# Order of the first rows of a Fourier layer, and operands of a seven-product matmul formed two steps sooner

## The chip, the cores and the metric

The kernel runs on one core of a Trainium2 chip. Its engines are TensorE (PE in the profile; PEld are its weight loads), VectorE (DVE), ScalarE (ACT), GpSimd (POOL), and SyncE (SP), which here only issues DMAs. Each takes its instructions in program order; they meet through semaphores. An engine that waits for one instruction does not pass to the next. The metric is the device time of one execution, in microseconds.

## The reference

Two sublayers, each with a layer norm, a modulation of the normalized rows, and a gated residual; S = 2048 rows, D = 512, F = 1792.

```
mod = silu(c) @ w_mod                      # six rows sa, ca, ga, sb, cb, gb
h = layernorm(x) * (1 + ca) + sa
a, b = h @ Wd_re.T, h @ Wd_im.T
x = x + ga * (Ws_re @ a - Ws_im @ b)       # Fourier mixing
h = layernorm(x) * (1 + cb) + sb
z = gelu(h @ w_in)                         # 512 -> 1792
z1, z2 = z[:, :896], layernorm(z[:, 896:])
g = w_sp @ z2 + b_sp                       # 2048 x 2048
x = x + gb * ((z1 * g) @ w_out)
```

All is float32.

## The kernel before

**Three products for one.** TensorE works on a reduced float type. Each operand is split into a high part (ScalarE copies it to that type) and a low part (VectorE subtracts the high part from the original). `matmul3` (L93 to L97) then makes three matmuls: high by high, and the two mixed ones. L95, L96 and L97 in the profile are these three. `ah` and `al` are the high and low parts of the streamed chunk (`prep_hi`, L289 for the high part; `prep_lo`, L307 for the low part); a chunk is 128 x 512.

**Order.** The order of every engine's instructions is written out by hand. The work counts through chunks n. For each, `prep(n)` emits the high part of chunk n+3 and the low part of chunk n+2, then come the matmuls, then what `at(n, ...)` has put on the list for n. N2 = 128 is the first chunk of z1, N3 the first of z2, N4 the first of the big product with w_sp.

**The head.** Stage one multiplies the normalized rows (without the modulation, which is folded into other operands) by the sequence matrices. A row block s of x (128 rows) becomes the stationary operand: `stats_first(s)` takes mean and variance on VectorE (L423 to L426) and then the power and the scaled shift on GpSimd (L427, L428, tile `first`). `norm_x(s)` makes the normalized rows `xn` on ScalarE (L119) after GpSimd has filled their column 0 with ones (L468). The high part `hh` comes in one of two ways. `hi_first(s)` makes it straight from x, with scale and shift inside one activation (L444), and then writes the one column of ones (L446). `hi_h(s)` copies it from `xn` (L477). `lo_h(s)` subtracts on VectorE: `hl` = xn - hh (L482). The streamed chunk is a 32 x 32-block transpose on VectorE of a block of the sequence matrix (`t`, L190, from `stage`). Block 0 holds chunks 0 to 3. Block 1, the first of the second matrix, holds chunks 4 to 7; its load is issued ahead of all this. For the first four chunks `mm_a` (L501) runs three passes of four matmuls: hh by ah, hh by al, hl by ah.

The head before gives row blocks 0 and 1 to `hi_first` and 2 and 3 to `hi_h`.

**z1 with seven products.** The product of h with the left half of `w_in` uses a seven-product scheme (Strassen's, in Winograd's form) over two halves of the features and two halves of the rows. Four quarters g of 512 rows each have four chunks of 128 features: `TT[k, g]`. Half gg pairs quarter gg with quarter 2+gg. With a = TT[kk, gg], b = TT[2+kk, gg], c = TT[kk, 2+gg] and d = TT[2+kk, 2+gg] the scheme needs the difference a - c and S2 = d - (a - c), and later a + S2 (`sum_x11`) and b - S2 (`sum_x12`). Products run in the order 1, 2, 6, 7, 4, 5, 3, each in two steps of two chunks, one for each half: step n (even) uses chunks n and n+1. A step has 18 matmuls into three banks (`z1p`). Product 6 uses S2, product 7 uses a + S2, product 5 uses the difference, which lies where c was.

Around a step, in the program's order (`mm_z1`): the matmuls; the high parts of the two chunks four ahead (`ahead`); the emptying of the banks. For product 1 and for 6 and 7 the emptying is a copy (L772). For product 2 it is, for each bank, a gelu out of it (L731, `z1o`) and a refill with product 1 (L759, `z1p<-z`). After that stand the low parts of the same two chunks. The weights of product p are formed by `form_v`, split by `hi_v` (L658) and `lo_v` (L662), and kept in two buffers `vj`.

The left half has 896 columns: 2 x 384 go through the scheme, the last 128 (`f7p`, weights `w7`) are multiplied plainly. For quarters 2 and 3 this needs the original c in high and low parts (`make_x`: `xh` L218, `xl` L221). `mm_x` runs these 12 matmuls, 6 behind step 6 and 6 behind step 12.

**Where these things lie and when.** The quarters 2 and 3 are loaded by `load_t` (L209) into numbered slots of 2 KB per partition, a pool opened at the start of z1 where the Fourier stage's weight pool (`htpool`: 19 tiles of 2 KB and one of 0.5 KB) and its neighbours were. Before, in `make_x(0)` xh and xl of half 0 lie in slots 9 to 12, and VectorE alternates: xl, difference, xl, difference. The difference goes into the slot of c (L223). `form_t` forms S2 (L245) inside `prep_hi`, that is directly ahead of the high part of the chunk that uses it: two chunks of four ahead of product 6's step. For half 1, `make_d` (L234) writes the differences into the buffers `bh`, `bl` of a third pool at step 6.

Stores of finished z1 rows (`z_d<-z1o`, L734) are issued by GpSimd. The copies of product 6 go into the buffers of product 2's rows once they are stored. Loads of w_sp blocks (`sj`, L833) are issued by SP from step 6 on.

Of the kernel before, what the change touches and what calls it, by code (L numbers as in the profile page):

```python
# [8 lines left out]
F32 = mybir.dt.float32  # L9
F32R = mybir.dt.float32r  # L10
AF = mybir.ActivationFunctionType
ALU = mybir.AluOpType

P = 128
# [5 lines left out]
def fnet_gmlp_kernel(  # L20
# [32 lines left out]
    nc = tc.nc  # L53
# [3 lines left out]
    Q = 512  # L57
# [5 lines left out]
    x = x.rearrange("b s d -> (b s) d")  # L63
# [59 lines left out]
    def at(n, f, *a):  # L123
        fill.setdefault(n, []).append((f, a))
# [14 lines left out]
    N2 = 4 * len(src)  # L139
# [61 lines left out]
    def slot(i, name, dtype=F32):  # L201
        return slots[0].tile([P, Q], dtype, tag=f"slot{i}", bufs=1, name=name)
# [3 lines left out]
    def load_t(g):  # L206
        for k in range(ND):
            TT[k, g] = slot(1 + 4 * (g - 2) + k, f"tt{g}_{k}")
            nc.sync.dma_start(TT[k, g], ht_d[g][k * P:(k + 1) * P, :])  # L209

    def make_x(gg):

        if gg:
            XH[gg] = [[bpool[0].tile([P, Q], F32R, tag=m, bufs=3, name=f"x{m}{kk}") for m in ("bh", "bl")] for kk in range(2)]
        else:
            XH[gg] = [(slot(9 + kk, f"xh{gg}{kk}", F32R), slot(11 + kk, f"xl{gg}{kk}", F32R)) for kk in range(2)]
        for kk, (h, _) in enumerate(XH[gg]):
            nc.scalar.activation(h, TT[kk, 2 + gg], AF.Copy)  # L218
        for kk, (h, l) in enumerate(XH[gg]):
            t = TT[kk, 2 + gg]  # L220
            nc.vector.tensor_tensor(l, t, h.bitcast(F32), op=ALU.subtract)  # L221
            if not gg:
                nc.vector.tensor_tensor(t, TT[kk, gg], t, op=ALU.subtract)  # L223
        if gg:
            for kk in range(2):
                TT[kk, 3] = XD[kk]

    XD = []

    def make_d():  # L230

        for kk in range(2):
            XD.append(bpool[0].tile([P, Q], F32, tag=("bh", "bl")[kk], bufs=3, name=f"xd{kk}"))
            nc.vector.tensor_tensor(XD[kk], TT[kk, 1], TT[kk, 3], op=ALU.subtract)  # L234

    def form_t(n):

        stage1 = n < N3
        p = (YPROD if stage1 else ZPROD)[(n - (N2 if stage1 else N3)) // 4]
        gg, kk = divmod(n % 4, 2)  # L240
        a, b, c, d = TT[kk, gg], TT[2 + kk, gg], TT.get((kk, 2 + gg)), TT.get((2 + kk, 2 + gg))
        if p == 6:
            if stage1:
                S2[gg, kk] = slot(13 + 2 * gg + kk, f"s2_{gg}{kk}")
                nc.vector.tensor_tensor(S2[gg, kk], d, XD[kk] if gg else c, op=ALU.subtract)  # L245
            return S2[gg, kk]
        if stage1:
            return {1: a, 2: b, 7: a, 4: b, 5: c, 3: d}[p]
        if p in (1, 2):
            t = blocks.tile([P, Q], F32, tag="t", bufs=2, name=f"t{n}")  # L250
            nc.vector.tensor_tensor(t, a if p == 1 else b, S2[gg, kk], op=ALU.subtract if p == 1 else ALU.add)
            return t
        return {7: c, 4: d, 5: a, 3: b}[p]
# [18 lines left out]
    def prep_hi(n):  # L272
        if n >= NE or n in highs:
            return
        highs.add(n)
        if N2 <= n < N4:
            T[n] = form_t(n)
        else:
            b, k = divmod(n, 4) if n < N2 else (NB0 + (n - N4) // 4, (n - N4) % 4)
            if b != NB0:  # L280
                T[n] = blocks.tile([P, Q], F32, tag="t", bufs=2, name=f"t{n}")
            if b == NB0:
                assert n in T
            elif n >= N4:
                squares(T[n], stage[b][:, k % 2], k // 2)
            else:
                squares(T[n], stage[b], k)
        AH[n] = SE[2][:, n - N4] if N4 <= n < N4 + 4 else blocks.tile([P, Q], F32R, tag="ah", bufs=4, name=f"ah{n}")
        nc.scalar.activation(AH[n], T[n], AF.Copy)  # L289
        if not N2 <= n < N4 and k == 3:  # L290
            stage.pop(b)
            if b != NB0:
                load(b + 2)


    def prep_lo(n):
        if n >= NE or n in lows:
            return
        lows.add(n)
        if N2 <= n < N4 and n % 4 == 3:  # L300
            AL[n] = slot(0, f"al{n}", F32R) if slots else zrow[0].tile([P, Q], F32R, tag="z1u", bufs=6, name=f"al{n}")
        elif N4 <= n < N4 + 4:
            AL[n] = slot(9 + n - N4, f"al{n}", F32R)
        else:
            AL[n] = blocks.tile([P, Q], F32R, tag="al", bufs=3, name=f"al{n}")
        t = T.pop(n)
        nc.vector.tensor_tensor(AL[n], t, AH[n].bitcast(F32), op=ALU.subtract)  # L307
# [112 lines left out]
    def stats_first(s):  # L420

        m = spool.tile([P, 12], F32, tag="first", bufs=4, name=f"first{s}")
        nc.vector.bn_stats(m[:, :6], X[s])  # L423
        mv = m[:, 8:]
        nc.vector.bn_aggr(mv[:, :2], m[:, :6])
        nc.vector.tensor_scalar(mv[:, 1:2], mv[:, 1:2], EPS, None, op0=ALU.add)  # L426
        nc.gpsimd.tensor_tensor(mv[:, 2:3], mv[:, 1:2], mhalf, op=ALU.pow)  # L427
        nc.gpsimd.tensor_scalar(mv[:, 3:4], mv[:, 0:1], mv[:, 2:3], -1.0, op0=ALU.mult, op1=ALU.mult)  # L428
        NRM[s] = mv[:, 2:3], mv[:, 3:4]
# [11 lines left out]
    def hi_first(s):  # L441
        h_hi[s] = hpool.tile([P, ND, P], F32R, name=f"hh{s}")
        h = h_hi[s].rearrange("p k (a i) -> p k a i", i=32)
        nc.scalar.activation(h, X[s].rearrange("p (a k i) -> p k a i", a=4, i=32), AF.Identity,  # L444
                             bias=NRM[s][1], scale=NRM[s][0])
        nc.scalar.activation(h_hi[s][:, 0, :1], ones[:, :1], AF.Copy)  # L446
# [16 lines left out]
    def norm_x(s):  # L463

        if s not in LN:
            LN[s] = spool.tile([P, D], F32, tag="xn", bufs=4, name=f"xn{s}")
        if s > 1:
            nc.gpsimd.memset(LN[s][:, 0:1], 1.0)  # L468
        apply(LN[s][:, 1:], X.pop(s)[:, 1:], NRM.pop(s))
# [5 lines left out]
    def hi_h(s):  # L475
        h_hi[s] = hpool.tile([P, ND, P], F32R, name=f"hh{s}")
        nc.scalar.activation(*parts_h(s, h_hi), AF.Copy)  # L477

    def lo_h(s):
        h_lo[s] = hpool.tile([P, ND, P], F32R, name=f"hl{s}")  # L480
        lo, h = parts_h(s, h_lo)
        nc.vector.tensor_tensor(lo, h, parts_h(s, h_hi)[0].bitcast(F32), op=ALU.subtract)  # L482
        LN.pop(s)
# [172 lines left out]
    def hi_v(p):  # L656
        WJ[1, p] = wpool[0].tile([P, 2, 2, Q], F32R, tag="wj", bufs=2, name=f"vj{p}")
        nc.scalar.activation(WJ[1, p][:, 0, :, :FM], v_of(p), AF.Copy)  # L658
# [56 lines left out]
    def end_f7(g):  # L715
        end_z1(g, NF - 1, ZT.pop(("f7", g)), out_row(g, NF - 1))
# [23 lines left out]
    def mm_z1(n):  # L740
        p = YPROD[(n - N2) // 4]
        gg = n % 4 // 2
        fresh = p in (1, 5)
        a = [(AH.pop(m), AL.pop(m)) for m in (n, n + 1)]
        if p in (2, 3):
            for kk, t in enumerate(a):
                mm_f7(gg if p == 2 else 2 + gg, 2 + kk, *t)
        for f in range(3):
            if fresh:
                ZT[gg, f] = bank(3 * gg + f, f"z1p{p}_{gg}{f}")  # L750
            cols = slice(f * P, (f + 1) * P)
            for kk, (th, tl) in enumerate(a):
                matmul3(ZT[gg, f], WJ[1, p][:, 0, kk, cols], WJ[1, p][:, 1, kk, cols], th, tl,
                        fresh and kk == 0, kk == 1, not fresh)
        ahead(n)
        for f in range(3):
            empty_z1(p, gg, f)
            if p == 2:
                nc.scalar.activation(turned(ZT[gg, f]), natural(Z1.pop((1, gg, f))), AF.Copy)  # L759
        if p == 1:  # L760
            for kk, t in enumerate(a):
                mm_f7(gg, kk, *t)
        if p == 2 and gg:
            hi_v(7)
            end_f7(1)

    def empty_z1(p, gg, f):
# [249 lines left out]
    stats_first(1)  # L1017
    prep_lo(0)
    norm_x(0)
    hi_first(1)  # L1020
    prep_hi(1)
    lo_h(0)
    stats_first(2)
    prep_lo(1)
    norm_x(1)
    lo_h(1)
    norm_x(2)
    hi_h(2)
    prep_hi(2)
    stats_first(3)  # L1030
    norm_x(3)
    at(0, lo_h, 2)
    at(0, hi_h, 3)
    at(1, lo_h, 3)
    at(0, load_x, 1, range(2, 4))
    at(2, load_row)
# [7 lines left out]
    for s, n in ((4, 4), (5, 4), (6, 6), (7, 6), (8, 10), (9, 10)):  # L1044
        m = n + (s == 9)
# [117 lines left out]
    at(N2 + 1, load_wi, 1, 2)  # L1163
    at(N2 + 2, form_v, 6)
    at(N2 + 3, load_t, 3)
    at(N2 + 4, make_x, 0)
    at(N2 + 6, make_d)
    at(N2 + 8, sum_x11, 0)
    at(N2 + 10, sum_x11, 1)
    at(N2 + 12, sum_x12, 0)  # L1170
    at(N2 + 14, sum_x12, 1)
    at(N2 + 13, form_v, 5)
    at(N2 + 17, form_v, 3)
    for i, p in enumerate(YPROD[2:]):
        if p != 7:
            at(N2 + 4 + 4 * i - (not i), hi_v, p)
        at(N2 + 5 + 4 * i - 2 * (not i), lo_v, p)
    at(N2 + 10, make_x, 1)
    at(N2 + 20, form_w, 7)
    at(NY[3], hi_w, 1)  # L1180
    at(NY[3] + 1, lo_w, 1)
# [162 lines left out]
```

## Time and profile before

| | |
|---|---|
| median of 3 runs | 941.92 us (941.4 to 942.54) |
| the profiled execution | 941.69 us |
| its span, first to last instruction | 939.9 us |
| granted clock of TensorE | 1.000 |
| busy: TensorE, VectorE, ScalarE, GpSimd | 931.0, 737.3, 414.3, 195.9 us |
| z1 on the span's time axis | 448.2 to 519.4 us |

Times in rows are microseconds from the span's start, and the second number is the length. `x2` at the end of a row means two instructions of the same kind, merged. Square brackets give the idle time of the engine ahead of the instruction and what ended it. A row `A <- B: total, times, longest` is an engine that waited for another. A matmul is listed with the time until its last result; the next one starts earlier than that.

### The profile page before, as it was taken

Reading aid. Unit: us, or ns where it says so; the run is one execution under the profiler, and the core shown is the slowest. Engines: PE = TensorE matmul, PEld = TensorE weight load, DVE = VectorE, ACT = ScalarE, POOL = GpSimd, SP = SyncE. Lnnn points to the kernel's source line nnn. Section 1 sums busy time; section 2 is a strip of 40 time slices with the busy share of each in tenths; the row PEclk is TensorE's granted clock in tenths of the full one; section 3 lists DMA queues with packets and bytes.
Section 4 is the critical chain, followed back from the end, with each engine's and each line's share of the span. In section 5 each row is a group of like instructions: output and inputs, shape, how many; then the busy total and the mean of one; then the engine's idle time right before and its main releaser. Section 6 shows DMA issues by size and latency. Waiting matters only on the chain.

```text
span 939.9 us, 12367 instructions
## 1 busy us (share of the span) xinstructions
PE 931.0 (99%) x4112; PEld 771.6 (82%) x4112; DVE 737.3 (78%) x1203; ACT 414.3 (44%) x728; POOL 195.9 (21%) x370
## 2 busy tenths in 40 slices
PE   8999999999999999999999999999999999999998
PEld 5888888888888888888878999888888888888886
DVE  6789957778677677875889878899799889886662
ACT  5685424232132222222488678674545544331221
POOL 2330000114554165323424211332000000000000
PEclk9999999999999999999999999999999999999999
DMA  9995762647539977994777523344564466744551
GB/s 204 226 224 123 144 145 68 168 135 183 141 86 303 294 212 215 277 336 147 234 279 271 183 92 74 92 100 104 130 140 107 114 145 135 179 112 145 183 176 56
DMA packets 236656, 157.08 MB, mean 167 GB/s; under 512 B 131536, under 2 KB 203472, under 8 KB 236464
## 3 DMA queue, kind: packets, MB, share of 16 engines
q1 hardware_dynamic: 222016, 118.39, 50.9%
q0 software_dynamic: 12128, 37.11, 11.0%
q10 hardware_dynamic: 2448, 0.79, 0.3%
q8 instruction: 32, 0.52, 0.2%
q14 instruction: 32, 0.26, 0.1%
HBM read 119.54 MB, written 36.70 MB: 166 GB/s over the span
## 4 chain that ended last, share of the span: by engine, by line
PE 92%; DVE 3%; ACT 2%; issue 1%; POOL 1%; DMA 0%; ACTq 0%; DVEq 0%; POOLq 0%
PE gp L96 12%; PE gp L97 12%; PE gp L95 12%; PE gw L95 10%; PE gw L96 10%; PE gw L97 10%; PE op L97 3%; PE op L96 3%; PE op L95 3%; PE yp L97 3%; PE yp L95 3%; PE yp L96 3%; PE z2p L96 2%; PE z2p L97 2%; PE z2p L95 2%; PE z1p L97 1%
## 5 line engine op out<-in xcount | busy, mean ns | idle before, releaser
L289 ACT ACTIVATE ah<-t 128x512 fp32r<-128x512 f32 x244 | 154.0, 632 | 370.3 <-DVE t L190 244.0
L307 DVE TENSOR_TENSOR al<-t,ah 128x512 fp32r<-128x512 f32 x244 | 164.0, 673 | 63.5 <-PE gp L96 37.5
L95 PE MATMUL gp<-ah,hh 128*128 128x512 f32 x496 | 193.0, 389 | 0.0
L97 PE MATMUL gp<-ah,hl 128*128 128x512 f32 x496 | 193.0, 389 | 0.0
L96 PE MATMUL gp<-al,hh 128*128 128x512 f32 x496 | 192.9, 389 | 0.0
L190 DVE STREAM_TRANSPOSE t<-stage 128x512 f32<-128x512 f32 x236 | 165.8, 702 | 10.4 <-DMA stage<-in_A_dft_seq_re_dram 4.0
L96 PE MATMUL gw<-al,bh 128*128 128x512 f32 x400 | 155.6, 389 | 0.0
L97 PE MATMUL gw<-ah,bl 128*128 128x512 f32 x384 | 149.5, 389 | 0.0
L95 PE MATMUL gw<-ah,bh 128*128 128x512 f32 x384 | 149.4, 389 | 0.0
L95 PEld LDWEIGHTS gp<-ah,hh 128*128 128x128 f32 x496 | 93.1, 188 | 19.4
L97 PEld LDWEIGHTS gp<-ah,hl 128*128 128x128 f32 x496 | 93.1, 188 | 19.3
L96 PEld LDWEIGHTS gp<-al,hh 128*128 128x128 f32 x496 | 93.1, 188 | 19.3
L96 PEld LDWEIGHTS gw<-al,bh 128*128 128x128 f32 x400 | 75.1, 188 | 15.5
L97 PEld LDWEIGHTS gw<-ah,bl 128*128 128x128 f32 x384 | 72.1, 188 | 15.3 <-DVE bl L874 0.3
L95 PEld LDWEIGHTS gw<-ah,bh 128*128 128x128 f32 x384 | 72.1, 188 | 15.0
L846 POOL DMA_DIRECT2D s_d<-sj x64 | 35.1, 548 | 99.0 <-DVE sj L838 73.9
L95 PE MATMUL yp<-hth,gh 128*128 128x512 f32 x128 | 49.8, 389 | 0.0
L96 PE MATMUL yp<-htl,gh 128*128 128x512 f32 x128 | 49.8, 389 | 0.0
L97 PE MATMUL yp<-hth,gl 128*128 128x512 f32 x128 | 49.8, 389 | 0.0
L623 POOL DMA_DIRECT2D ht_d<-hturn x62 | 40.9, 665 | 23.6 <-DVE hturn L619 19.6
L95 PE MATMUL op<-woh,uh 128*128 128x512 f32 x112 | 43.6, 389 | 0.0
L96 PE MATMUL op<-wol,uh 128*128 128x512 f32 x112 | 43.6, 389 | 0.0
(222 smaller groups left out, 1464.3 us busy)
## 6 DMA issues: line engine op xcount, KB each, us to landing
stage<-in_A_dft_seq_im_dram SPq DMA_DIRECT2D x64, 256.0 KB, 5.4
sj<-in_B_w_sp_dram SPq DMA_DIRECT2D x32, 512.0 KB, 7.6
s_d<-sj POOLq DMA_DIRECT2D x64, 256.0 KB, 4.1
stage<-s_d SPq DMA_DIRECT2D x128, 128.0 KB, 2.9
stage<-in_A_dft_seq_re_dram SPq DMA_DIRECT2D x60, 256.0 KB, 5.5
stage<-in_B_w_sp_dram SPq DMA_DIRECT2D x88, 128.0 KB, 3.2
wm<-in_w_mod_dram SPq DMA_DIRECT2D x16, 256.0 KB, 5.7
xr<-in_A_x_dram POOLq DMA_DIRECT2D x16, 256.0 KB, 4.2
```

The costliest lines, as they stand in the source:

```text
L95: nc.tensor.matmul(acc, ah, bh, start=first, stop=False, skip_group_check=go_on)
L96: nc.tensor.matmul(acc, ah, bl, start=False, stop=False, skip_group_check=go_on)
L97: nc.tensor.matmul(acc, al, bh, start=False, stop=last, skip_group_check=go_on)
L190: nc.vector.transpose(dst.rearrange("p (b i) -> p b i", i=32), block[:, :, 32 * k:32 * k + 32])
L289: nc.scalar.activation(AH[n], T[n], AF.Copy)
L307: nc.vector.tensor_tensor(AL[n], t, AH[n].bitcast(F32), op=ALU.subtract)
L623: eng.dma_start(v[a, i], ht[32 * a:32 * a + 32].rearrange("c (b r) -> c b r", r=32))
L846: nc.gpsimd.dma_start(s_d[m, r, g][b * P:(b + 1) * P, :], a)
```

## The change

In the head, the high part of the next chunk is emitted ahead of the row block's high part, `hi_first` serves all four row blocks, and row 3's statistics and chunk 3's high part come before the loop begins.

In z1, `make_x` is taken apart. The differences have slots of their own (9 to 12, `make_d(gg)`), the originals are kept as `XR`, and S2 has a function of its own (`form_s2`). Differences and S2 of half 0 are emitted at N2+2 and N2+3, of half 1 at N2+6. xh and xl of both halves lie in the buffers `bh` and `bl`. `make_xl(0)` comes at N2+5, the low weights of product 6 at N2+4 and those of product 7 at N2+8 (one earlier). The gelu of quarter 1's last 128 columns (`end_f7(1)`) moves from behind step 6 to behind step 8.

```
+    def make_d(gg):
+        for kk in range(2):
+            XD[gg, kk] = slot(9 + 2 * gg + kk, f"xd{gg}{kk}")
+            XR[gg, kk] = TT[kk, 2 + gg]
+            nc.vector.tensor_tensor(XD[gg, kk], TT[kk, gg], XR[gg, kk], op=ALU.subtract)
+            TT[kk, 2 + gg] = XD[gg, kk]
...
     def make_x(gg):
-        if gg:
-            XH[gg] = [[bpool[0].tile([P, Q], F32R, tag=m, bufs=3, name=f"x{m}{kk}") for m in ("bh", "bl")] for kk in range(2)]
-        else:
-            XH[gg] = [(slot(9 + kk, f"xh{gg}{kk}", F32R), slot(11 + kk, f"xl{gg}{kk}", F32R)) for kk in range(2)]
+        XH[gg] = [[bpool[0].tile([P, Q], F32R, tag=m, bufs=3, name=f"x{m}{gg}{kk}") for m in ("bh", "bl")] for kk in range(2)]
         for kk, (h, _) in enumerate(XH[gg]):
-            nc.scalar.activation(h, TT[kk, 2 + gg], AF.Copy)
+            nc.scalar.activation(h, XR[gg, kk], AF.Copy)
+    def make_xl(gg):
         for kk, (h, l) in enumerate(XH[gg]):
-            t = TT[kk, 2 + gg]
-            nc.vector.tensor_tensor(l, t, h.bitcast(F32), op=ALU.subtract)
-            if not gg:
-                nc.vector.tensor_tensor(t, TT[kk, gg], t, op=ALU.subtract)
...
+            nc.vector.tensor_tensor(l, XR[gg, kk], h.bitcast(F32), op=ALU.subtract)
+
+    def form_s2(gg):
         for kk in range(2):
+            S2[gg, kk] = slot(13 + 2 * gg + kk, f"s2_{gg}{kk}")
+            nc.vector.tensor_tensor(S2[gg, kk], TT[2 + kk, 2 + gg], TT[kk, 2 + gg], op=ALU.subtract)
...
         if p == 2 and gg:
             hi_v(7)
+        if n == N2 + 8:
             end_f7(1)
...
     norm_x(0)
-    hi_first(1)
     prep_hi(1)
     lo_h(0)
+    hi_first(1)
     stats_first(2)
     prep_lo(1)
     norm_x(1)
+    prep_hi(2)
     lo_h(1)
+    hi_first(2)
+    stats_first(3)
+    prep_lo(2)
     norm_x(2)
-    hi_h(2)
-    prep_hi(2)
-    stats_first(3)
+    prep_hi(3)
+    hi_first(3)
     norm_x(3)
     at(0, lo_h, 2)
-    at(0, hi_h, 3)
...
-    at(N2 + 4, make_x, 0)
-    at(N2 + 6, make_d)
+    at(N2 + 2, make_d, 0)
+    at(N2 + 3, form_s2, 0)
+    at(N2 + 5, make_xl, 0)
+    at(N2 + 6, make_d, 1)
+    at(N2 + 6, form_s2, 1)
...
-    for i, p in enumerate(YPROD[2:]):
-        if p != 7:
-            at(N2 + 4 + 4 * i - (not i), hi_v, p)
-        at(N2 + 5 + 4 * i - 2 * (not i), lo_v, p)
+    at(N2 + 3, hi_v, 6)
+    at(N2 + 4, lo_v, 6)
+    at(N2 + 4, make_x, 0)
+    at(N2 + 8, lo_v, 7)
+    for i, p in enumerate(YPROD[4:]):
+        at(N2 + 12 + 4 * i, hi_v, p)
+        at(N2 + 13 + 4 * i, lo_v, p)
     at(N2 + 10, make_x, 1)
+    at(N2 + 10, make_xl, 1)
```

More of the change, by code (lines that the diff above doesn't have):

```diff
@@ L209, in load_t @@
             nc.sync.dma_start(TT[k, g], ht_d[g][k * P:(k + 1) * P, :])
+    XR, XD = {}, {}
+    def make_d(gg):
[4 more added lines that the diff above has]
+            TT[kk, 2 + gg] = XD[gg, kk]
     def make_x(gg):
-        if gg:
-            XH[gg] = [[bpool[0].tile([P, Q], F32R, tag=m, bufs=3, name=f"x{m}{kk}") for m in ("bh", "bl")] for kk in range(2)]
-        else:
-            XH[gg] = [(slot(9 + kk, f"xh{gg}{kk}", F32R), slot(11 + kk, f"xl{gg}{kk}", F32R)) for kk in range(2)]
+        XH[gg] = [[bpool[0].tile([P, Q], F32R, tag=m, bufs=3, name=f"x{m}{gg}{kk}") for m in ("bh", "bl")] for kk in range(2)]
         for kk, (h, _) in enumerate(XH[gg]):
-            nc.scalar.activation(h, TT[kk, 2 + gg], AF.Copy)
+            nc.scalar.activation(h, XR[gg, kk], AF.Copy)
+    def make_xl(gg):
         for kk, (h, l) in enumerate(XH[gg]):
-            t = TT[kk, 2 + gg]
-            nc.vector.tensor_tensor(l, t, h.bitcast(F32), op=ALU.subtract)
-            if not gg:
-                nc.vector.tensor_tensor(t, TT[kk, gg], t, op=ALU.subtract)
[L224 to L230, printed above, removed]
+            nc.vector.tensor_tensor(l, XR[gg, kk], h.bitcast(F32), op=ALU.subtract)
+    def form_s2(gg):
         for kk in range(2):
-            XD.append(bpool[0].tile([P, Q], F32, tag=("bh", "bl")[kk], bufs=3, name=f"xd{kk}"))
-            nc.vector.tensor_tensor(XD[kk], TT[kk, 1], TT[kk, 3], op=ALU.subtract)
+            S2[gg, kk] = slot(13 + 2 * gg + kk, f"s2_{gg}{kk}")
+            nc.vector.tensor_tensor(S2[gg, kk], TT[2 + kk, 2 + gg], TT[kk, 2 + gg], op=ALU.subtract)
     def form_t(n):
@@ L242, in form_t @@
         if p == 6:
-            if stage1:
-                S2[gg, kk] = slot(13 + 2 * gg + kk, f"s2_{gg}{kk}")
-                nc.vector.tensor_tensor(S2[gg, kk], d, XD[kk] if gg else c, op=ALU.subtract)
             return S2[gg, kk]
```

## The prediction

> **What bounds the kernel now.** The page comes first: where the time goes, whether the clock is full, which engine the chain runs through.
>
> ```profile
> span 939.9 us, 12367 instructions
> PEclk9999999999999999999999999999999999999999
> PE 92%; DVE 3%; ACT 2%; issue 1%; POOL 1%; DMA 0%; ACTq 0%; DVEq 0%; POOLq 0%
> ```
>
> TensorE carries 92% of the chain at full clock. Whatever the change does to other engines counts only where TensorE stands still. So the waits of TensorE come second:
>
> ```profile
> PE gp L501 <- ACT ah L289: 0.9, 2, 0.5
> PE z1p L95 <- ACT z1p L759: 0.8, 1, 0.8
> PE z1p L95 <- ACT z L772: 0.7, 1, 0.7
> PE z1p L97 <- DVE vj L662: 0.5, 1, 0.5
> PE gp L501 <- ACT hh L477: 0.4, 1, 0.4
> PE gp L501 <- DVE al L307: 0.2, 1, 0.2
> ```
>
> Apart from a start-up wait ahead of all work, these are all. They sit in two places, and the change touches both: the head (gp, L501) and z1 (z1p). Third, the stretch of z1 that holds the three waits, and the one behind it, as busy time by stretch (length, each engine's busy time, and last the granted clock, the DMA share and GB/s):
>
> ```profile
> 469.95:486.75 16.80, 14.80 (x61) 10.95 (x60) 12.54 (x21) 16.61 (x31) 3.79 (x7) 1.00 1.00 372
> 486.75:519.39 32.64, 32.64 (x145) 27.04 (x144) 30.38 (x46) 23.03 (x41) 13.42 (x25) 1.00 0.61 228
> ```
>
> The second stretch has 144 matmuls (count by weight loads) in 32.64 us: 0.2267 us each when nothing waits. The first has 60, which would take 13.60; it takes 16.80. So z1 has 3.20 us to give, waits and slow restarts together. ScalarE (fourth engine number) is busy 16.61 of these 16.80: it is the bound there.
>
> **z1, step by step.** The rows that show why ScalarE is late:
>
> ```profile
> 461.49 0.96 DVE L647 TENSOR_TENSOR w1e<-w 128x768 f32<-128x768 f32 x1
> ...
> 465.35 1.16 ACT L218 ACTIVATE xh<-tt 128x512 fp32r<-128x512 f32 x2
> 466.39 0.60 ACT L731 ACTIVATE z1o<-f7p 128x512 f32<-128x512 f32 x1
> ...
> 469.04 1.28 DVE L245 TENSOR_TENSOR s<-tt,tt 128x512 f32<-128x512 f32 x2
> 469.83 1.23 ACT L289 ACTIVATE ah<-s 128x512 fp32r<-128x512 f32 x2 [2.83 <-DVE s L245]
> ...
> 471.59 0.60 ACT L759 ACTIVATE z1p<-z 128x512 f32<-128x512 f32 x1
> ...
> 472.74 0.60 ACT L759 ACTIVATE z1p<-z 128x512 f32<-128x512 f32 x1
> ...
> 478.92 0.83 ACT L658 ACTIVATE vj<-w 128x768 fp32r<-128x768 f32 x1
> ...
> 481.17 1.07 ACT L772 ACTIVATE z<-z1p 128x512 f32<-128x512 f32 x2
> ```
>
> The high parts of S2 (ah<-s) stand in ScalarE's order ahead of the emptying of product 2, and waited 2.83 us for VectorE to form S2, behind the xl and difference pairs. TensorE then waited for the first z1p refill (471.59+0.60 is 472.19). Everything ScalarE did from there to the z copies at 481.17 was that much late.
>
> Pitches for the ledger: a VectorE 128x512 pair takes 1.28, so 0.61 per instruction and 0.68 until its result; ScalarE's ah and xh 0.52 and 0.64 (1.16 a pair); a z1o with its z1p 1.15 (471.59 to 472.74); a z copy 0.48 and 0.59.
>
> - The differences of half 0 (xd, two) now follow w1e, from 462.45: al of chunks 6, 7 end at 464.35 and 464.96. This is the one new delay, 1.22 at most. TensorE wants al6 at 464.74 (24 matmuls ahead of 469.95 is 464.51, plus one) and al7 at 465.42. Cover 0.4; past it each us costs one.
> - S2 of half 0 (two, from 464.87) is done at 466.1. The low part of product 6's weights follows, until 467.05. ScalarE does xh and z1o<-f7p as now, then finds S2 ready: hi of chunks 8, 9 from 466.9 instead of 469.83, no wait. Gain on ScalarE 2.9.
> - Product 2's first half is emptied from 467.95: the first z1p ends at 469.2, the last at 471.5. TensorE wants the first at 469.95 + 6 x 0.2267 = 471.31. The 0.8 wait goes, with 2.1 to spare.
> - al8, al9 (467.6), xl of half 0 (moved behind them, 468.8 to 470.1): the extra-row matmuls want the second xl at 470.86. Cover 0.7.
> - Half 1's differences and S2: 470.0 to 472.5. They read the quarter that lands last; see the rows below. hi of chunks 10, 11 from 472.0, the second emptying from 473.1, its first z1p at 474.35, wanted at 471.31 + 18 x 0.2267 = 475.39. ScalarE stands some 0.5 idle, the last slack it has.
> - High part of product 7's weights (0.83) at 476.6; hi12, hi13 from 477.3; the z copies from 478.3, the first done at 478.9. TensorE wants it at 479.47. The 0.7 wait goes with 0.5 to spare. VectorE's low part of those weights, now ahead of al12 and al13, ends at 478.4 and is wanted at 479.9: the 0.5 wait goes.
> - The gelu of quarter 1's last 128 columns moves behind the z copies: same 0.6, off that path.
> - xh, xl of half 1 and product 4's low weights come out at 482.2 and 488.2, wanted at 483.78 and about 489.4. So no wait is late next; TensorE reaches the stretch that began at 486.75 at 483.55.
>
> Sum for z1: -3.20. No DMA is added or moved in any engine's order. But the z1 rows are stored 2 to 3 us sooner, beside loads that already fill the engines (DMA share 1.00 in the first stretch). The rows for that: time to landing of the last quarter's loads, the later two of four (issued by 466.6), and of the row store issued at 467.29.
>
> ```profile
> tt<-ht_d SPq DMA_DIRECT2D x2, 256.0 KB, 4.4
> ...
> z_d<-z1o POOLq DMA_DIRECT2D x1, 256.0 KB, 7.3
> ```
>
> The last quarter is there at 471.0; S2 of half 1 first needs its last chunk at 471.85. Product 6's copies reuse the buffers whose rows are stored from 468.6; at 7.3 they are free at 475.9, wanted at 478.3. Both are covered, and I cost them at nothing; the upper ends stand with the rivals.
>
> **The head.** Here the chain before runs hh3, then twelve matmuls:
>
> ```profile
> 1.53 5.68 PE L389 MATMUL busyp<-busy,ones 128*128 128x512 f32 x8 [1.53 <-DVE busy L328]
> ...
> 5.08 0.34 PEld L389 LDWEIGHTS busyp<-busy,ones 128*128 128x128 f32 x1 [0.52 <-issue]
> ...
> 5.69 0.27 POOL L428 TENSOR_SCALAR first<-first 128x1 f32<-128x1 f32 x1
> ...
> 5.76 0.19 PEld L389 LDWEIGHTS busyp<-busy,ones 128*128 128x128 f32 x1 [0.35 <-issue]
> ...
> 9.81 0.81 ACT L444 ACTIVATE hh<-x,first 128x512 fp32r<-128x512 f32 x1 [1.54 <-POOL first L428]
> ...
> 10.50 0.15 DVE L426 TENSOR_SCALAR first<-first 128x1 f32<-128x1 f32 x1
> ...
> 14.57 0.55 POOL L427 TENSOR_TENSOR first<-first,mhalf 128x1 f32<-128x1 f32 x1 [2.38 <-DVE first L426]
> ...
> 15.22 1.11 POOL L428 TENSOR_SCALAR first<-first 128x1 f32<-128x1 f32 x1
> ...
> 15.73 1.19 PE L501 MATMUL gp<-al,hh 128*128 128x512 f32 x4 [0.22 <-DVE al L307]
> ...
> 16.36 0.82 ACT L119 ACTIVATE xn<-x,first 128x511 f32<-128x511 f32 x1 [2.11 <-POOL xn L468]
> ...
> 16.77 1.08 PE L501 MATMUL gp<-ah,hl 128*128 128x512 f32 x4
> ...
> 17.72 0.71 DVE L190 STREAM_TRANSPOSE t<-stage 128x512 f32<-128x512 f32 x1 [1.44 <-DMA stage<-in_A_dft_seq_im_dram]
> ...
> 18.35 0.65 DVE L307 TENSOR_TENSOR al<-t,ah 128x512 fp32r<-128x512 f32 x1
> ...
> 19.30 1.07 PE L501 MATMUL gp<-al,hh 128*128 128x512 f32 x4
> ...
> 21.12 0.39 PE L95 MATMUL gp<-ah,hh 128*128 128x512 f32 x1
> ```
>
> The order up to 10.65 (end of L426 for row 2) stays on VectorE. From there, in the new order and by about 0.65 each: al1 to 11.35, t2 to 12.0, hl1 to 12.6, the statistics of row 3 (1.1) to 13.7, al2 to 14.3, t3 to 14.9. GpSimd: the power of row 3 (0.55) behind al2 to 14.85, its scaling (0.27) to 15.15, and only then the one-column fill of xn2, which stood ahead of row 3's statistics before. ScalarE: xn2 (0.82) to 16.05, ah3 to 16.4, hh3 straight from x (0.81) to 17.1; hl2 ends at 16.75. If xn2 need not wait for that fill, all this comes about 1 sooner. So chunk 3 starts between 16.6 and 17.9, against 18.27. ScalarE's two longer activations and two one-column writes, under 1 us, lie in time in which it waits.
>
> But VectorE's order stays t4, al3, hl3. t4 transposes the first block of the second matrix, cannot start before that lands (17.72), and its load is not moved. al3 still ends at 19.00. Chunk 3's second pass starts at 19.05 instead of 19.30, and behind a stop: such a pass takes 1.04 (15.73 to 16.77), one without 0.91. Its last pass then starts at 20.1 and chunk 4 at 21.0 instead of 21.12.
>
> Gain 0.1, of the 1.5 us of waits that the head shows. The ends are 0.25 of gain (no slow restart) and 0.3 of loss. The loss would come from GpSimd: its scaling took 0.27 with no subtraction on VectorE and 1.11 beside al and hl. Were row 3's that long again, hl2 would end at 17.6, chunk 3's first pass run from 18.6 to 19.5, and chunk 4 start at 21.4. I take 0.1, because beside that scaling the new order has the transpose t3 and no subtraction.
> The Trainium skill (SBUF — State Buffer, section SBUF: two separate sides) says that VectorE and GpSimd share a port pair as an exclusive lock, which a VectorE operation with two SBUF inputs takes. The trace agrees (0.27 against 1.11); by that rule the order of the two engines decides between the two ends.
>
> **Sum.** -3.20 - 0.1 = -3.3 us. The profiled execution took 941.69 (span 939.9), 0.23 below the median 941.92. 941.69 - 3.3 = 938.4; on the median's side 938.6. I take 938.5.
>
> **Rivals.**
> - *Part of it comes back as a new wait in z1.* al6 is the tightest edge. If the first write of half 0's differences had to wait for memory that the closed pools leave, until the last transposed rows are stored (about 465.2, when the last quarter's loads could begin), al6 would end at 467.1 and TensorE lose 2.4: 940.9. A shorter hold costs less: 939.3 to 940.9. Against it: by the code the seventeen slots of 2 KB fit within what the closed weight pool held, which at its end only TensorE and VectorE still read.
> - *ScalarE remains the bound and nothing is gained.* 16.61 of 16.80 busy speaks for it. Against: the work counted there began late; 2.9 us of it now falls before 469.95. Time 941.8.
> - *Slower: the row buffers.* Product 6's copies wait for the stores of product 2's rows. With a landing of 7.3 nothing; from about 10.3 on, each us is one on ScalarE and on TensorE; from 13.5 the change loses. At 15.5 it gives 943.8. For it: DMA share 1.00. Against: no store there is seen above 7.3.
> - *The clock falls in the head.* TensorE would stand still 0.3 to 1.4 us before al3, perhaps longer than any stop there now (0.5). At half rate (weight load 0.34, as at 5.08, against 0.19 at 5.76) for the 4.2 us that the start needed, from the first matmul at 1.53 to about 5.7, it loses 2.1: 940.6. The Trainium skill (TensorE: Matmul & The Clock Gate, What's actually happening) has the clock fall only after a whole idle window of about 3.4 us; by that rule this costs nothing. The trace agrees so far: full clock in every slice in spite of the stops.
>
> **How the numbers follow.** Forecast 938.5, chance 0.70, own range 937.9 to 939.3 (the head's ends, and some 0.7 if the last quarter lands 1.5 later, which is past its cover and past the z copies' 0.5). Part back 0.13, nothing gained 0.07, slower 0.05, clock 0.05. A measurement of this kernel can tell about 0.2%, 1.9 us, from no change: faster is below 940.0. That holds the forecast and half of part back: 0.77. Same: the other half, nothing gained, the clock: 0.18. Slower 0.05. The range 937.6 to 940.7 leaves out nothing gained, slower and the far end of part back.
>
> **What would show it.** In the profile after: no TensorE wait in z1 (the stretch between the two extra-row groups is 13.6 long); ah<-s some 2.9 sooner against the z1 start, without a wait on s; ScalarE near 80% busy there; in the head a TensorE wait on al L307 of 0.3 to 1.4 us that ends at 19.05, and chunk 4 at 21.0. Wrong would be: a wait on ah or al at the start of product 2's second half, a ScalarE wait on a store, a head in which hl2 ends after 17.0, or t4 that starts elsewhere than 17.7.

## The result, and the profile after

The changed kernel takes 938.92 us (median of 7; six lie between 938.35 and 939.23, one at 941.03) against 941.71 (median of 7, 941.4 to 942.54): a ratio of 0.9972, 95% interval 0.996 to 0.9983. That is 2.8 us less, where 938.5 and 3.3 less than the profiled execution were forecast. The profiled execution after took 939.23 us, its span 937.4.

The waits of TensorE in the changed kernel (waiting line, what it waited for, us in total, times, longest):

```profile
PE busyp L387 <- DVE busy L326: 1.5, 1, 1.5
PE gp L499 <- DVE al L305: 1.4, 1, 1.4
PE gp L499 <- ACT ah L287: 0.4, 1, 0.4
```

All three waits of z1 are gone. In the head one long wait on al stands where several short ones were. The two stretches of z1, from the first extra-row group to the second and from there to the end of z1 (length, busy time of PE, PEld, DVE, ACT, POOL, then clock, DMA share, GB/s):

```profile
470.74:484.34 13.60, 13.60 (x61) 11.26 (x60) 11.00 (x19) 12.99 (x25) 3.25 (x6) 1.00 1.01 358
484.34:516.98 32.64, 32.64 (x145) 27.03 (x144) 30.43 (x46) 23.64 (x42) 13.47 (x25) 1.00 0.74 273
```

The first was 16.80 long and is 13.60 now: the whole 3.20 came, and the stretch behind it has its old length, so nothing was given back. The stretch starts at 470.74, though, and not at 469.95. All of those 0.79 us are there already at the end of the head. The timeline of the head after:

```profile
6.77 0.71 DVE L190 STREAM_TRANSPOSE t<-stage 128x512 f32<-128x512 f32 x1 [1.85 <-DMA x<-in_A_x_dram]
...
14.22 0.80 ACT L119 ACTIVATE xn<-x,first 128x511 f32<-128x511 f32 x1
...
15.38 0.27 POOL L426 TENSOR_SCALAR first<-first 128x1 f32<-128x1 f32 x1
...
15.59 0.13 POOL L466 MEMSET xn<- 128x1 f32 x2
...
15.72 0.69 DVE L480 TENSOR_TENSOR hl<-xn,hh 128x512 fp32r<-128x512 f32 x1 [0.22 <-POOL xn L466]
...
17.50 1.07 PE L499 MATMUL gp<-ah,hh 128*128 128x512 f32 x4
...
18.64 0.71 DVE L190 STREAM_TRANSPOSE t<-stage 128x512 f32<-128x512 f32 x1 [2.23 <-DMA stage<-in_A_dft_seq_im_dram]
...
19.27 0.65 DVE L305 TENSOR_TENSOR al<-t,ah 128x512 fp32r<-128x512 f32 x1
...
19.98 1.20 PE L499 MATMUL gp<-al,hh 128*128 128x512 f32 x4 [1.41 <-DVE al L305]
21.92 0.39 PE L95 MATMUL gp<-ah,hh 128*128 128x512 f32 x1
```

Chunk 3 starts at 17.50, sooner than the 18.27 of before. Then TensorE stands for 1.41 us until al3 is there, because al3 (19.27) stands behind t4 (18.64), which waited for its load. In this execution t4 (the transpose for chunk 4, at 18.64) is 0.9 later than the 17.72 of before, and so was the very first transpose (6.77 against 5.88). Whether the new order does that, or the loads land when they like, is the first question for the experiments.

### The profile page after: what moved, and what is told of

Its sections match the earlier page's. It is cut to its first block, busy times and chain, and to the rows that moved or that the text cites. A ratio compares the mean times of both kernels' runs of the same rounds, so it can differ in the third digit from the quotient of the medians.

```text
span 937.4 us, 12369 instructions
## 1 busy us (share of the span) xinstructions
PE 930.2 (99%) x4112; PEld 772.1 (82%) x4112; DVE 737.4 (79%) x1203; ACT 415.4 (44%) x730; POOL 194.5 (21%) x370
## 4 chain that ended last, share of the span: by engine, by line
PE 97%; DMA 1%; SPq 1%; issue 0%; ACTq 0%; DVE 0%; ACT 0%; DVEq 0%
PE gp L95 12%; PE gp L97 12%; PE gp L96 12%; PE gw L97 10%; PE gw L96 10%; PE gw L95 10%; PE yp L97 3%; PE yp L96 3%; PE yp L95 3%; PE op L97 3%; PE op L95 3%; PE op L96 3%; PE z2p L97 2%; PE z2p L95 2%; PE z2p L96 2%; PE z1p L97 2%
```

## The experiments

### Each half of the change alone, and the changed kernel once more

z1_only takes the head of before and everything else of after; head_only the other way round.

```
 # head_only: these lines of after, all else of before (z1_only: the reverse)
     norm_x(0)
     prep_hi(1)
     lo_h(0)
     hi_first(1)
...
     hi_first(3)
     norm_x(3)
     at(0, lo_h, 2)
```

> The head of the kernel before, z1 of the changed kernel. Theory (the gain is z1's, 3.2 us; the head gives nothing that can be told): 938.5 us, the stretch of z1 between the two extra-row groups 13.6 us, no TensorE wait there. Rival (the later chunk 4 in the changed kernel's profile, 21.92 against 21.12, is a cost of the new head order): 938.5 too, but then the changed kernel stands 0.8 above it, and the first transpose here starts near 5.9.

> The head of the changed kernel, z1 of the kernel before. Theory (the new head is worth 0.1, because al3 stands behind the transpose of block 1; the start varies from run to run by where the first loads land): 941.6 us, al3's pass starting 1.3 us behind the start of that transpose, chunk 4 starting 3.3 us behind it (3.4 before). Rival (the new order itself costs 0.8 at the start): 942.5, with the first transpose at 6.8 again and before's at 5.9.

> The changed kernel once more, for where its first transpose starts (6.77 in its first profile, 5.88 in that of before). Theory (that is the landing of the first loads, which the change does not touch): somewhere between 5.8 and 6.8, not tied to the order; time 938.4 to 939.3, moving with it. Rival (the new order delays it): 6.7 to 6.9 again.

Measured, on one chip beside 16 runs of before (median 941.64):

| kernel | median us (runs) | ratio to before, 95% interval | z1 stretch us |
|---|---|---|---|
| z1_only | 938.75 (5) | 0.9969, 0.9956 to 0.9981 | 13.60 |
| head_only | 941.71 (11) | 1.0, 0.9991 to 1.0009 | 16.84 |
| after_again | 938.82 (6) | 0.9968, 0.9956 to 0.998 | 13.60 |

The z1 half carries the gain, and the head half is worth nothing that can be measured. The rival (the new head costs 0.8) falls: head_only stands at 941.71 and not at 942.5.

What moves the start is seen by the first transpose, t4 and chunk 4 in all ten profiles (start in us; chunk 4 is its first matmul):

| profile | head | first transpose | t4 | chunk 4 | chunk 4 behind t4 |
|---|---|---|---|---|---|
| before | old | 5.88 | 17.72 | 21.12 | 3.40 |
| z1_only | old | 5.85 | 17.68 | 21.09 | 3.41 |
| tail (below) | old | 6.09 | 17.79 | 21.42 | 3.63 |
| before_again | old | 6.49 | 18.54 | 21.83 | 3.29 |
| after | new | 6.77 | 18.64 | 21.92 | 3.28 |
| after_again | new | 6.03 | 18.42 | 21.72 | 3.30 |
| head_only | new | 6.34 | 18.32 | 21.61 | 3.29 |
| s2_late (below) | new | 5.96 | 17.83 | 21.12 | 3.29 |
| al6_late (below) | new | 5.96 | 17.79 | 21.08 | 3.29 |
| al3_first (below) | new, al3 ahead of t4 | 6.14 | 17.96 | 19.66 | 1.70 |

before_again is the kernel before, run once more (942.65 us, one run):

> The kernel before once more, for where its first transpose starts (5.88 in its first profile, 5.85 in the run with its head; 6.03 to 6.77 in the four with the new head). Theory (the landing of the first loads varies whatever the order behind it): 5.8 to 6.8. Rival (the new order delays it): 5.8 to 5.9.

The old head starts its first transpose anywhere from 5.85 to 6.49, the new one from 5.96 to 6.77, and t4 from 17.7 to 18.6 in both. So the landing varies by up to 0.9 us, and no order behind it stands apart. Measured from t4, the new head is 3.28 to 3.30 as long as al3 stands behind t4. The old one is 3.40 to 3.63 where t4 comes 11.70 to 11.84 behind the first transpose, and the same 3.29 where it comes 12.05 behind (before_again: there, too, chunk 3's first pass is done before al3 comes). By these few profiles the head half gives 0.1 to 0.3 where block 1 lands soon after block 0, and nothing where it lands later.

### What caps the head

al3_first puts al3 and hl3 ahead of t4 in VectorE's order, in the changed kernel.

```
     at(0, lo_h, 2)
-    at(1, lo_h, 3)
+    at(0, prep_lo, 3)
+    at(0, lo_h, 3)
```

> The changed kernel with al3 and hl3 ahead of the transpose of block 1 in VectorE's order. Theory (what caps the head is that al3 stands behind that transpose): the 1.4 us wait on al3 goes; TensorE next waits for al4, which needs two transposes after the landing; chunk 4 starts about 1.9 us behind the start of the transpose instead of 3.3; 1.2 to 1.4 us faster than the changed kernel, 937.3. Rival (the landing itself caps the head): same time as the changed kernel, 938.7, the wait moved to ah of chunk 4.

Measured: 937.43 us (5 runs, 937.22 to 938.29), ratio to before 0.9956, 0.9944 to 0.9969; 1.4 below after_again on the same chip. It is the fastest version here. Its timeline at that place:

```profile
15.76 0.68 DVE L305 TENSOR_TENSOR al<-t,ah 128x512 fp32r<-128x512 f32 x1
...
17.35 0.69 DVE L480 TENSOR_TENSOR hl<-xn,hh 128x512 fp32r<-128x512 f32 x1 [0.91 <-ACT xn L119]
...
17.84 1.07 PE L499 MATMUL gp<-al,hh 128*128 128x512 f32 x4
17.96 1.30 DVE L190 STREAM_TRANSPOSE t<-stage 128x512 f32<-128x512 f32 x2
...
19.44 0.69 DVE L305 TENSOR_TENSOR al<-t,ah 128x512 fp32r<-128x512 f32 x1 [0.17 <-ACT ah L287]
19.66 0.40 PE L95 MATMUL gp<-ah,hh 128*128 128x512 f32 x1
...
20.18 0.19 PEld L96 LDWEIGHTS gp<-al,hh 128*128 128x128 f32 x1 [0.54 <-DVE al L305]
20.18 0.50 PE L96 MATMUL gp<-al,hh 128*128 128x512 f32 x1
...
20.75 0.40 PE L95 MATMUL gp<-ah,hh 128*128 128x512 f32 x1
```

al3 is formed at 15.76, before the load has landed, and chunk 3's three passes run without a stop. Chunk 4 starts 1.70 behind t4 (19.66 less 17.96). Its second matmul then waits for al4 (the weight load at 20.18), and its fourth starts at 20.75 where 0.68 behind the first would be 20.34: 0.41 lost, so 2.11 in effect against 3.29. The theory holds: the wait on al3 was what capped the head. The chain of waits in this kernel shows what is late next:

```profile
12.30 5.54 DMA stage<-in_A_dft_seq_im_dram
...
17.96 0.72 DVE t L190
...
18.77 0.64 ACT ah L287
...
19.44 0.70 DVE al L305
...
20.18 0.50 PE gp L96
```

By that chain the landing itself (17.84) is now the bound, through t4, ah4 and al4. But hl3, which stands ahead of t4, comes hardly sooner: VectorE goes from hl3 (17.35, after a wait of 0.91 on xn3) to t4 without a stop. An earlier load of block 1 was not tried, and in this execution it would have met hl3 at once.

### Which part of the z1 edit carries the 3.2

tail is the kernel before with two of the edits only; S2 stays where it was.

```
             hi_v(7)
+        if n == N2 + 8:
             end_f7(1)
...
-        at(N2 + 5 + 4 * i - 2 * (not i), lo_v, p)
+        at(N2 + 5 + 4 * i - 2 * (not i) - (p == 7), lo_v, p)
```

> The kernel before with only two of the edits of z1: the gelu of quarter 1's last columns behind step 8, and the low weights of product 7 one step sooner. S2 stays where it was. By the same ledger: the wait on the first z1p refill stays (0.8), the wait on the z copies is shorter by one ScalarE instruction (0.5), the wait on the low weights goes (0.7 with its restart). Stretch between the extra-row groups 15.6 us instead of 16.8, time 940.5. Rival (the sooner S2 carries all of the 3.2): 16.6 to 16.8, time 941.6.

Measured: 940.96 us (10 runs; before 941.85 in 19 on that chip), ratio 0.9992, 0.9983 to 1.0002. The total alone can't be told from no change, but the stretch can:

```profile
470.24:485.97 15.73, 14.52 (x62) 11.03 (x60) 12.34 (x20) 15.51 (x29) 3.79 (x7) 1.00 1.02 393
```

Its TensorE waits in z1, from the same profile:

```profile
PE z1p L95 <- ACT z1p L759: 0.9, 1, 0.9
...
PE z1p L95 <- ACT z L773: 0.2, 1, 0.2
```

15.73 against 16.80: the two small moves alone bring 1.07 of the 3.20. The wait on the low weights is gone, the one on the z copies is down from 0.7 to 0.2, the one on the refill stays. The rest of the edit (differences and S2 formed sooner, xl behind them) brings the other 2.1 on top of them. What it would bring without them was not run.

s2_late keeps everything of after, but forms S2 of half 0 behind the xl, as before.

```
-    at(N2 + 3, form_s2, 0)
-    at(N2 + 5, make_xl, 0)
...
     at(N2 + 4, make_x, 0)
+    at(N2 + 4, make_xl, 0)
+    at(N2 + 4, form_s2, 0)
```

> The changed kernel with S2 of half 0 formed behind the xl of half 0 (the order it had before), all else as changed. By the ledger S2 comes 2.0 later on ScalarE than in the changed kernel, 0.9 sooner than before; the z1p refills still come in time, the z copies come 0.3 late: stretch 14.0 us instead of 13.6. Rival (S2 sooner is the whole of it): 15 to 16 us.

Measured in one run (939.0 us), its stretch:

```profile
469.95:483.86 13.91, 13.89 (x61) 11.19 (x60) 10.79 (x18) 13.75 (x26) 3.79 (x7) 1.00 1.02 359
```

13.91, where 14.0 was expected and the rival wanted 15 to 16. (The high parts of S2 start at 468.17, 1.3 later than the ledger has them in the changed kernel; the 2.0 in the expectation was too much.) With the other edits in place the exact place of S2 costs 0.3, and it falls where it was expected, at the first z copy:

```profile
479.65 0.50 PE L95 MATMUL z1p<-ah,vj 128*128 128x512 f32 x1
```

By the prediction TensorE wants this matmul at 479.47; it comes 0.18 late, and the next follows after 0.34 instead of 0.23. So the two small moves are not the whole of it, and S2 ahead of the xl is not either. What the sooner differences bring by themselves was not measured.

al6_late tests the edge that the prediction held for the tightest. The two differences are formed a second time, ahead of al6.

```
+    def again(gg):
+        for kk in range(2):
+            nc.vector.tensor_tensor(XD[gg, kk], TT[kk, gg], XR[gg, kk], op=ALU.subtract)
...
     at(N2 + 2, make_d, 0)
+    at(N2 + 2, again, 0)
```

> The changed kernel with half 0's differences formed twice, so that al6 ends 1.2 later. The prediction gave al6 a cover of 0.4 and each us past it one: a TensorE wait of about 0.85 on al in the first extra-row group of step 6, time 0.9 above the changed kernel (939.7); the stretch behind stays 13.6. Rival (VectorE's order has more slack there than the ledger says): no wait, 938.8.

Measured: 939.71 us (10 runs), ratio 0.9977, 0.9967 to 0.9986. The wait, and the stretch from the group that waits to the end of the one behind it:

```profile
464.47 0.39 PE L95 MATMUL f7p<-ah,w 128*128 128x512 f32 x1
...
464.74 1.28 DVE L310 TENSOR_TENSOR al<-xb,ah 128x512 fp32r<-128x512 f32 x2
...
465.48 0.50 PE L96 MATMUL f7p<-al,w 128*128 128x512 f32 x1 [0.63 <-DVE al L310]
```

```profile
470.86:484.46 13.60, 13.60 (x61) 11.26 (x60) 11.02 (x19) 12.50 (x24) 2.69 (x5) 1.00 1.00 363
464.47:470.86 6.39, 5.76 (x25) 4.42 (x24) 6.39 (x11) 6.29 (x13) 1.68 (x3) 1.00 0.64 215
```

The 24 matmuls from 464.47 to 470.86 would take 5.44 and take 6.39: 0.95 lost. al6 starts at 464.74, 1.21 later than in z1_only (463.53, with the same group at 464.46). The matmul that needs it would follow 0.23 behind 464.47, at 464.70, and starts at 465.48, 0.78 late. So 0.4 of the delay was covered, as predicted, and the rest was paid. The other 0.17 goes with the slow start behind the stop. The changed kernel shows the same margin: al6 is done at 465.07 (464.39 and 0.68), and its matmul starts at

```profile
465.53 0.39 PE L96 MATMUL f7p<-al,w 128*128 128x512 f32 x1
```

## Why the prediction was right

**The bound and the 3.20.** Right to the hundredth: the stretch is 13.60. The ledger can be held against the rows after, shifted by the 0.79 that the stretch began later:

```profile
464.39 1.29 DVE L305 TENSOR_TENSOR al<-xb,ah 128x512 fp32r<-128x512 f32 x2
465.60 1.29 DVE L235 TENSOR_TENSOR s<-tt,xd 128x512 f32<-128x512 f32 x2
...
467.65 1.17 ACT L287 ACTIVATE ah<-s 128x512 fp32r<-128x512 f32 x2
...
469.33 0.60 ACT L757 ACTIVATE z1p<-z 128x512 f32<-128x512 f32 x1
...
472.72 1.24 ACT L287 ACTIVATE ah<-s 128x512 fp32r<-128x512 f32 x2 [0.48 <-DVE s L235]
...
478.19 0.96 DVE L660 TENSOR_TENSOR vj<-w,vj 128x768 fp32r<-128x768 f32 x1 [2.30 <-ACT vj L656]
...
479.10 1.55 ACT L771 ACTIVATE z<-z1p 128x512 f32<-128x512 f32 x3
```

| step | forecast us | after, less 0.79 |
|---|---|---|
| S2 of half 0 done | 466.1 | 466.10 |
| hi8 starts | 466.9 | 466.86 |
| first z1p refill ends | 469.2 | 469.14 |
| hi10 starts, behind ScalarE's last idle time | 472.0, 0.5 | 471.93, 0.48 |
| low weights of product 7 end | 478.4 | 478.36 |
| first z copy starts | 478.3 | 478.31 |

Pitches from the trace of before, laid end to end in the new order of each engine, were good to 0.1 us over 16 us.

**The head.** The mechanism was right, and its place too: one wait on al3, 1.41 (0.3 to 1.4 were given), ended 1.34 behind the start of t4 (1.33 by the prediction), GpSimd's scaling 0.27 as taken. The two cases left open are decided: xn2 (14.22) does not wait for its one-column fill (15.59); hl2 does (the 0.22 at 15.72). The term of 0.1 is too small for the totals to show: head_only stands at 941.71 against 941.64. What the prediction named as a sign of being wrong did come, t4 at 18.64 and not at 17.7. The table above puts that on the landing of the load. The prediction treated a landing as fixed from one profile; it varies from one execution to the next, in both kernels.

**The rivals.** Part back: no wait on memory showed at the first differences; they follow w1e at once. Nothing gained: ScalarE is no longer the bound. But the sign that I gave for it was wrong: its busy share in the stretch is 96% (12.99 of 13.60), not near 80%. The ledger could have said so. 16.61 less the 2.9 that moves ahead of the stretch is 13.7, which is near 80% of the old length, but all of the new one. One more instruction moved out behind it (ScalarE's second stretch is busy 23.64 instead of 23.03). The sign that counts is not the share but that TensorE no longer waits for ScalarE. The clock did not fall with a stop of 1.41 us: the granted clock is 1.000 after. The Trainium skill's rule (TensorE: Matmul & The Clock Gate, section What's actually happening) of a whole idle window of about 3.4 us agrees with that.

The slower rival came nearer than the prediction's cover suggests. The stores do take longer to land: 8.1 to 8.5 us, where the same three took 6.6 to 6.9 before. They are now issued sooner, beside the loads of w_sp; that this is the cause is likely, but no run separates it. For the three row blocks of product 2's first half, issue by GpSimd and time to landing:

```profile
469.59 0.55 POOL L732 DMA_DIRECT2D z_d<-z1o  x1 [0.94 <-ACT z1o L729]
470.74 0.54 POOL L732 DMA_DIRECT2D z_d<-z1o  x1 [0.60 <-ACT z1o L729]
471.90 0.54 POOL L732 DMA_DIRECT2D z_d<-z1o  x1 [0.61 <-ACT z1o L729]
```

```profile
z_d<-z1o POOLq DMA_DIRECT2D x1, 256.0 KB, 8.5
...
z_d<-z1o POOLq DMA_DIRECT2D x1, 256.0 KB, 8.2
...
z_d<-z1o POOLq DMA_DIRECT2D x1, 256.0 KB, 8.1
```

Free at 478.1, 478.9 and 480.0; the three z copies start at 479.10, 479.58 and 480.06. The cover of 2.4 that I had worked out with 7.3 was 1.0 for the first and next to nothing for the third. By the ledger TensorE wants the third two banks later, so a little more would still have cost nothing.

The other cover on a landing was thin too. The prediction has the last quarter there at 471.0, wanted at 471.85. In s2_late it took 5.4 to land instead of 4.4, and S2's last chunk waited for it:

```profile
472.19 0.69 DVE L235 TENSOR_TENSOR s<-tt,xd 128x512 f32<-128x512 f32 x1 [0.25 <-DMA tt<-ht_d]
```

ScalarE was later than that there, so it cost nothing.

**The sum.** 3.3 was forecast, 2.8 is the difference of the medians; with z1_only at 938.75 against 941.64 it is 2.9 for z1 alone. The stretch says 3.20 exactly. Counted from chunk 4 on, the profiled executions agree with it: 941.69 less 21.12 is 920.57 before, 938.41 less 21.09 is 917.32 in z1_only, and 939.23 less 21.92 is 917.31 after. What the medians lack of it lies ahead of chunk 4, where executions differ by up to 0.8; how the runs without a profile started is not known.

## What to carry to other kernels

Where engines run fixed lists, take the pitches from one trace, write each engine's new list end to end, and compare each result with the moment at which the bounding engine wants it: the gain and the margins between engines both fall out, here to 0.1 us. Margins against a landing do not: a cover of 2.4 shrank to next to nothing, and one of 0.85 was used up in one run. A chain shortened ahead of a fixed arrival gives nothing while something that is needed sooner still stands behind the arrival in an engine's order; move that ahead first (1.4 us here, for two moved lines). And a bound that is to vanish needs every late step on its engine moved: the two small moves alone brought 1.07 of 3.20, and all but the best place for S2 brought 2.9.

## What the runs showed of the hardware

The first loads of a run land at times that differ between executions: by up to 0.9 us over the ten profiles (first transpose at 5.85 to 6.77, t4 at 17.68 to 18.64), and by 0.6 to 0.7 for the first transpose between two executions of the same kernel (before 5.88 and 6.49, after 6.77 and 6.03). SP's issue shows it as well. Its waits for the first block's loads, in the first 12 us of before and of after:

```profile
SPq L413 <- DMA stage<-in_A_dft_seq_re_dram: 1.2, 2, 1.0
```

```profile
SPq L411 <- DMA stage<-in_A_dft_seq_re_dram: 2.0, 2, 1.0
```

SP issues block 1's load behind that. In program order it stands ahead of all work of the head, but on the time axis it begins here, before and after:

```profile
10.52 2.02 SPq L155 DMA_DIRECT2D stage<-in_A_dft_seq_im_dram  x4
```

```profile
11.40 2.02 SPq L155 DMA_DIRECT2D stage<-in_A_dft_seq_im_dram  x4
```

t4 starts 7.1 to 7.4 behind that moment in all ten profiles, so its 0.9 is mostly that of SP's issue. What decides how long the first block takes stays open. A gain of a tenth in the head can't be read from one profile; it has to be measured from the landing on.
